# Three more mirrored score blocks per batch through VectorE, a planned number of score pairs per step, and casting loads of v and z

## The chip, the cores and the metric

The kernel runs on one core of one Trainium2 chip. The metric is the device time of one execution in microseconds, as the median of several runs. TensorE does the matrix products, VectorE, ScalarE and GpSimd (POOL in the profile) the elementwise work, and DMA queues, of which SyncE's (SP) is the main one, the loads, stores and transposes.

## The reference, cut to what matters

Two blocks follow each other, for 8 batches of 3200 tokens with 256 features.

```python
# u, v: (8, 3200, 256), z: (8, 3200, 64), all float32
scores = (1 / S) * z @ z.transpose(0, 2, 1)      # (8, 3200, 3200), symmetric
attn = np.maximum(scores, 0) ** 2                # symmetric too
x = u * (attn @ v)                               # (8, 3200, 256)

wq, wk = x @ w_q, x @ w_k                        # (8, 3200, 64)
W_tok = (1 / 8) * einsum('bsd,btd->bst', wq, wk)
mixed = einsum('bst,btd->bsd', W_tok, x)         # linear: wq @ (wk.T @ x)
out = np.maximum(mixed, 0) @ w_out
```

The score matrix is symmetric, so a block of it that is computed once can serve a second time as its transpose.

## The kernel before, in words

**Tiles.** A batch has 25 row tiles of 128 tokens (`NT`) and seven column groups: six of 512 tokens and a last one of 128 (`widths`, `NG`, `LASTG`). A score tile is 128 rows by 512 columns in fp16 for one row tile `ti` and one group `gi`; in the narrow group up to four row tiles share one. The list `tiles` holds all of them in the order in which they are made, and `ends` says where a group's tiles end. `is_turned(gi, gj)` says that the block of group `gi` with the four row tiles of group `gj` is made once and its mirror image, the block of `gj` with the rows of `gi`, comes by transposing. Ten blocks of a batch are such: those with `gj` at most two groups after `gi`, and (0, 4). The tiles of the mirror images are left out of `tiles`.

**A score pair.** Two tiles are made together by `scores` (L274): each contracts over 64 features of z, so one runs on the lower and one on the upper half of TensorE's rows, into one PSUM tile of two banks. There are three such PSUM tiles (`pps`), and projections, mixes and outputs take theirs from the same three. `first_stage` (L294) applies the relu and a scale into an fp32 tile `g`, on VectorE or ScalarE; `second_stage` (L304) squares it into the fp16 tile `at`, on POOL or ScalarE. For tiles of a turned block, `second_stage` also issues a DMA transpose from SP's queue (L329) into a tile `tt`.

**The second product.** `second_product` (L442) accumulates attn @ v for one group in two PSUM banks, reading its left operand from `at` or `tt` (`weights`, L434). When a group closes, `gate` (L466) multiplies by u into `x_sb`. Projections, heads, mixes and output products of the second block (`projections`, `heads`, `mix`, `proj_items`) are slipped between.

**Steps.** The main loop (L943) runs in steps `k`. Each step makes score pairs for later use, squares those of the step before (`waiting`), and does a part of the second product of the current group with tiles made at least `LAG` = 2 steps earlier. The loop makes three pairs per step, or two when a mix is done. How many rows of the second product a step takes follows from a heuristic at L1018 to L1032. One fixed pair of a step has its first stage on ScalarE (`act_pair`), the others on VectorE; of the second stages, fixed ones go to ScalarE. Each engine runs its instructions in the order in which they are written here.

**Loads.** The opening casts the first batch's v on the way by DMAs from POOL's queue (`load_first_v`, L111). For later batches `load_piece` (L140) loads pieces of v and z as fp32 by SP's queue into one of three staging tiles, and four or five steps later POOL or ScalarE, in turn, casts them to fp16 (L147):

```python
        def cast():
            copy = nc.gpsimd.tensor_copy if now[0] % 2 == 0 else nc.scalar.copy
            copy(out=dst()[:, n0 : n0 + nn, :], in_=piece[:])
```

`group_begun` (L794) says in which steps these loads are issued. The opening and the ending are written out by hand as lists of words.

Of the kernel before, what the change touches and what calls it, by code (L numbers as in the profile page):

```python
# [9 lines left out]
FP16 = mybir.dt.float16  # L10
# [6 lines left out]
def kernel(  # L17
# [31 lines left out]

    NAT = 11  # L50

    consts = ctx.enter_context(tc.tile_pool(name="consts", bufs=1))
# [86 lines left out]

    def load_piece(k, b, src, dst, n0, nn, later):  # L140
        d = src.shape[2]
        piece = pst.tile([P, nn, d], FP32, tag="piece", name="piece")
        nc.sync.dma_start(out=piece[:], in_=rows(src, b)[:, n0 : n0 + nn, :])

        def cast():
            copy = nc.gpsimd.tensor_copy if now[0] % 2 == 0 else nc.scalar.copy
            copy(out=dst()[:, n0 : n0 + nn, :], in_=piece[:])  # L147

        due(k + later, lambda: asides.append(cast))

    def load_v(k, b, n0, nn):
        if n0 == 0:
            vs[b] = pv.tile([P, NT, D], FP16, tag="v_sb", name="v_sb")
        load_piece(k, b, v, lambda: vs[b], n0, nn, 4 if b == 1 else 5)

    def load_z(k, b, n0, nn):
        load_piece(k, b, z, lambda: zr, n0, nn, 4)

# [18 lines left out]
    def spread_z(b, half, n0, n1):  # L177
        low, high = slice(0, dqk), slice(dqk, P)
        if half == 0:
# [53 lines left out]
    def is_turned(gi, gj):  # L233
        return gi < gj < LASTG and (gj <= gi + FAR or (gi, gj) == (0, 4))

# [58 lines left out]
    def first_stage(p0, sc, on_act):  # L294
        g = pg.tile([P, 2, W], FP32, tag="g", name="g")
        if on_act:
            nc.scalar.activation(out=g[:], in_=sc[:], func=RELU, scale=GSCALE)  # L297
        else:
            nc.vector.tensor_scalar(  # L299
                out=g[:], in0=sc[:], scalar1=0.0, scalar2=GSCALE, op0=AOP.max, op1=AOP.mult  # L300
            )
        return g

    def second_stage(p0, g, on_act):  # L304
        at = pat.tile([P, 2 * W], FP16, tag="at", name="at")
        out = at[:].rearrange("p (a w) -> p a w", a=2)
        if on_act:
            nc.scalar.square(out=out, in_=g[:])  # L308
        else:
            nc.gpsimd.tensor_mul(out=out, in0=g[:], in1=g[:])  # L310
# [7 lines left out]
        if len(blocks) == 2 and blocks[0][:3] == blocks[1][:3] and blocks[1][3] == blocks[0][3] + 1:  # L318
            blocks = [blocks[0][:4] + (2, blocks[0][5], blocks[1][6])]
        for b, gi, gj, n0, nn, c0, c1 in blocks:  # L320
            if (b, gi, gj) not in turned:
                bufs = {1: 3, 2: 4, 4: 1}[gj - gi]
                turned[b, gi, gj] = ptt.tile(
                    [P, 4, 4, P], FP16, tag=f"tt{gj - gi}", name=f"tt{gj - gi}", bufs=bufs
                )
# [5 lines left out]
        return turns  # L331

    accs = {}
# [132 lines left out]
    def gate(b, gi):  # L466
# [6 lines left out]
        ug = us.pop((b, gi))[:].rearrange("p n d -> p (n d)")  # L473
        n = min(2, nn) * D
        if is_split(b, gi):
            both = pg.tile([P, 2, W], FP32, tag="g", name="gt")
# [39 lines left out]
    def projections_out(b, gi, out):  # L516
        gw = widths[gi]
        if gi < LASTG:
            qks[b, gi] = pq.tile([P, W], FP16, tag="qk", name="qk")
        else:  # L520
            qks[b, gi] = pq.tile([P, P], FP16, tag="ql", name="ql", bufs=2)
        nc.scalar.copy(out=qks[b, gi][:, 0:gw], in_=out)  # L522

    def turn_keys(b, gi):
# [25 lines left out]

    def heads_out(b, gis, ps):
        if gis[0] == 0:
            hacc[b] = psml.tile([P, D], FP32, tag="ha", name="ha")
# [8 lines left out]

    def spread_heads(b):
        nc.scalar.copy(out=hss[b][dh:P, :], in_=hss[b][0:dh, :])
        nc.scalar.copy(out=hz[b % 2][dh:P, :], in_=hss[b][0:dh, :])
# [43 lines left out]
    def mix_out(b, pair, db, ps, on_dve=False):  # L609
        if db == 0:  # L610
# [3 lines left out]
            rts[b, pair, "both"] = both  # L614
        out = rts[b, pair, "both"][:, :, db, :]
        if on_dve:
            nc.vector.tensor_scalar(
# [46 lines left out]
    def proj_out(b, gi, src, ways):  # L664
# [8 lines left out]
        for on_dve, queue, n in ways:  # L673
            sl = slice(at * D, (at + n) * D)
            part = src[at // 2][:, 0 : n * D] if isinstance(src, list) else src[:, sl]
            if on_dve:
# [117 lines left out]
    def group_begun(k, b, gi):  # L794
# [4 lines left out]
        if gi == 0 and b + 1 < B:  # L799
            for i, (n0, nn) in enumerate([(0, 16), (16, NT - 16)]):  # L800
                at = k + (5 if b == 0 else 1) + i
                due(at, lambda at=at, n0=n0, nn=nn: load_z(at, b + 1, n0, nn))
            for i, n0 in enumerate((0, 5, 9)):
# [9 lines left out]
            for i in range(-(-NT // 4)):  # L813
                at = k + (9 + 5 * i // 3 if b == 0 else 4 + 2 * i)
                due(at, lambda at=at, i=i: load_v(at, b + 1, 4 * i, min(4, NT - 4 * i)))

# [29 lines left out]
    def key_due(k):  # L846
# [8 lines left out]
        begin = k + steps - 1  # L855
        if not todo_proj and not todo_mix and begin - k < 3 and begin - keyed_at[0] > 3:
# [80 lines left out]
    group_begun(1, 0, 0)  # L937
    steps = 6
    across = False
    left, first_sizes = [], [4, 5, 5, 5]  # L940
    gate_pending = False
    ahead = []
    while groups:  # L943
# [11 lines left out]
        if mix_due(k):  # L955
# [4 lines left out]
        n = min(n, NTILE - produced)  # L960
        pairs = list(range(produced, produced + n, 2))
        on_lanes = k >= 3 and len(pairs) + bool(mixing) >= 2
        keying = not mixing and key_due(k)
# [16 lines left out]
        staged = []  # L980
        act_pair = 0 if (gate_pending or k < 4) else 1
# [7 lines left out]
        if len(waiting) == 3:  # L989
            second_on_act = [False, True, k % 2 == 0]  # L990
        else:
            second_on_act = [False, True]
        seconds = [(p0, g, a) for (p0, g), a in zip(waiting, second_on_act) if g is not None]
        acts = [x for x in seconds if x[2]]
# [17 lines left out]
        if begins:  # L1012
# [4 lines left out]
            left = [t for t in range(NT) if t not in scored]  # L1017
        need = ends[b, gi]  # L1018
        rest = len(left) + sum(len(tis) for _, _, tis in tiles[consumed:need])
        if first_sizes:  # L1020
            size = first_sizes.pop(0)
            steps = len(first_sizes) + 1
        else:
            soon = [ready, made_by[k - 1], produced, produced + 5]
            steps = max(sum(need > x for x in soon) + 1, -(-rest // (25 if gi == LASTG else 13)))
            size = -(-rest // steps)
        closes = steps == 1
        new = min(ready, ends[b, gi]) - consumed
        if not closes:
            most = size + 3 if gi == LASTG else size  # L1030
            while new and sum(len(x[2]) for x in tiles[consumed : consumed + new]) > most:
                new -= 1  # L1032
        rows_ = [t for _, _, tis in tiles[consumed : consumed + new] for t in tis]
# [14 lines left out]
        if on_lanes:  # L1048
# [50 lines left out]
            todo = [(x, lambda lead, p0=p0: stage(p0, scores(p0, lead))) for x, p0 in zip(at_, between_)]  # L1099
# [161 lines left out]
```

## Time and profile before

| | |
|---|---|
| median of 3 runs | 778.56 us (778.5 to 779.31) |
| span of the profiled execution, first to last instruction | 776.9 us |
| TensorE busy | 765.0 us (98%) |
| VectorE / ScalarE / POOL busy | 474.0 / 558.4 / 554.1 us |
| granted TensorE clock, mean | 0.998 |

The profiled execution has no time of its own beside its span; the median of the runs stands 1.66 us above that span. In the groups of the profile a line reads: line, engine, operation, output tile, input tile, shapes, number of instructions, then busy microseconds, mean nanoseconds of one, and the idle time of the engine before them with what ended it.

### The profile page before, as it was taken

The numbers are of one execution on the slowest core, as the hardware profiler recorded it, in microseconds if no ns is written. First come the engines' busy times: TensorE is split into PE (matmuls) and PEld (weight loads), VectorE is DVE, ScalarE is ACT, GpSimd is POOL, SyncE is SP. The second block draws the span as 40 slices with busy tenths as digits, with TensorE's granted clock in tenths as the row PEclk, the third lists the DMA queues.
The fourth block names the chain that finished last, engine by engine and source line by source line (L and its number), as shares of the span: only waits on it lengthen the run. The fifth ranks groups of instructions, "written<-read, shape, count | busy, mean of one in ns | idle before, by whom it ended". The sixth has DMA issues, their size and how long they took to land.

```text
span 776.9 us, 28324 instructions
## 1 busy us (share of the span) xinstructions
PE 765.0 (98%) x12542; PEld 629.3 (81%) x12542; DVE 474.0 (61%) x459; ACT 558.4 (72%) x657; POOL 554.1 (71%) x361
## 2 busy tenths in 40 slices
PE   9999999999999999999999999999999999999996
PEld 6777877888788988888888887888888888988884
DVE  7654676546765577555766457655585646665444
ACT  8666787777778787685867667758687878685465
POOL 7897797768766678766879668886777546875450
PEclk9999999999999999999999999999999999999999
DMA  8899799987999679994999949999489995987726
GB/s 186 176 202 227 141 212 173 191 181 125 213 220 216 133 188 204 234 229 134 189 224 231 220 131 203 226 202 242 115 210 187 217 236 112 206 190 160 161 65 259
DMA packets 276554, 147.03 MB, mean 189 GB/s; under 512 B 252112, under 2 KB 255696, under 8 KB 276432
## 3 DMA queue, kind: packets, MB, share of 16 engines
q1 hardware_dynamic: 275712, 143.33, 87.8%
q0 software_dynamic: 576, 1.64, 1.1%
q8 instruction: 98, 1.61, 0.9%
q14 instruction: 24, 0.20, 0.1%
q10 hardware_dynamic: 144, 0.26, 0.1%
HBM read 59.38 MB, written 26.21 MB: 110 GB/s over the span
## 4 chain that ended last, share of the span: by engine, by line
PE 92%; DVE 2%; ACT 2%; POOL 1%; DMA 1%; issue 1%; ACTq 0%; DVEq 0%; POOLq 0%
PE acc L347 67%; PE sc L285 12%; PE qk L347 6%; PE fo L347 5%; PE mx L600 1%; POOL at L310 1%; DMA tt<-at 1%; DVE g L299 1%; DVE x_sb L485 1%; ACT at L308 1%; DVE fo L1219 0%; ACT g L297 0%; DMA z<-in_z_dram 0%; ACT gt L484 0%; DVE zT L136 0%
## 5 line engine op out<-in xcount | busy, mean ns | idle before, releaser
L299 DVE TENSOR_SCALAR g<-sc 128x1024 f32<-128x1024 f32 x337 | 410.1, 1223 | 242.1 <-PE sc L285 220.8
L310 POOL TENSOR_TENSOR at<-g 128x1024 f16<-128x1024 f32 x238 | 448.1, 1893 | 122.2 <-DVE g L299 93.6
L347 PE MATMUL acc<-v_sb,at 64*128 64x256 f16 (+1 forms) x7387 | 479.5, 269 | 2.0 <-DVE x_sb L485 0.7
L347 PEld LDWEIGHTS <-at 64*128 64x128 f16 (+1 forms) x7387 | 370.2, 94 | 84.3 <-PE acc L347 24.5
L308 ACT ACTIVATE at<-g 128x1024 f16<-128x1024 f32 x230 | 239.3, 1055 | 27.2 <-DVE g L299 16.0
L347 PE MATMUL acc<-v_sb,tt 64*128 64x256 f16 (+1 forms) x2540 | 179.2, 269 | 0.0
L285 PE MATMUL sc<-zT 64*128 64x512 f16 (+1 forms) x1104 | 170.3, 345 | 0.9 <-DVE g L299 0.5
L297 ACT ACTIVATE g<-sc 128x1024 f32<-128x1024 f32 x131 | 134.1, 1023 | 41.6 <-PE sc L285 39.5
L347 PEld LDWEIGHTS <-tt 64*128 64x128 f16 (+1 forms) x2540 | 129.5, 94 | 15.2
L487 POOL TENSOR_TENSOR x_sb<-gt,u_sb 128x512 f16<-128x512 f32 x48 | 61.2, 1275 | 71.5 <-ACT gt L484 56.6
L621 ACT ACTIVATE rt<-mx 128x1024 f16<-128x1024 f32 x47 | 47.9, 1024 | 30.8 <-PE mx L600 30.5
L285 PEld LDWEIGHTS <-zT 64*128 64x128 f16 x1104 | 57.3, 94 | 10.9 <-issue 3.2
L484 ACT COPY gt<-acc 128x512 f32<-128x512 f32 x48 | 28.1, 586 | 48.4 <-PE acc L347 48.2
L347 PE MATMUL fo<-wo,rt 64*128 64x256 f16 (+1 forms) x688 | 58.6, 270 | 0.0
L347 PE MATMUL qk<-x_sb,kx 64*128 64x256 f16 x368 | 55.7, 269 | 0.6 <-DVE g L299 0.6
L522 ACT CAST qk<-qk 128x512 f16<-128x512 f32 x47 | 27.5, 585 | 35.9 <-PE qk L347 35.8
L485 DVE TENSOR_TENSOR x_sb<-acc,u_sb 128x512 f16<-128x512 f32 x48 | 33.1, 690 | 26.1 <-PE acc L347 24.7
L347 PEld LDWEIGHTS <-rt 64*128 64x128 f16 (+1 forms) x688 | 36.6, 94 | 14.3 <-PE fo L347 5.2
L682 ACT ACTIVATE fo<-fo 128x1024 f32<-128x1024 f32 x39 | 39.9, 1023 | 4.3 <-PE fo L347 4.3
L347 PEld LDWEIGHTS <-kx 64*128 64x128 f16 (+1 forms) x386 | 35.7, 94 | 5.1 <-PE qk L347 0.2
L347 PE MATMUL qk<-xT_sb,wqk 64*128 64x512 f16 (+1 forms) x94 | 27.9, 377 | 0.0
L347 PE MATMUL qk<-xT_sb,wkq 64*128 64x512 f16 (+1 forms) x90 | 26.7, 376 | 0.4 <-ACT g L297 0.4
(79 smaller groups left out, 243.3 us busy)
## 6 DMA issues: line engine op xcount, KB each, us to landing
u_sb<-in_u_dram SPq DMA_DIRECT2D x48, 512.0 KB, 5.1
out_dram<-fo SPq DMA_DIRECT2D x43, 512.0 KB, 3.5
piece<-in_v_dram SPq DMA_DIRECT2D x42, 512.0 KB, 4.6
piece<-in_z_dram SPq DMA_DIRECT2D x7, 512.0 KB, 5.3
tt<-at SPq DMA_TRANSPOSE x162, 4.8
out_dram<-fo SPq DMA_DIRECT2D x9, 256.0 KB, 3.1
piece<-in_z_dram SPq DMA_DIRECT2D x7, 288.0 KB, 6.1
u_sb<-in_u_dram SPq DMA_DIRECT2D x8, 128.0 KB, 3.1
```

What stands on the lines that cost most here:

```text
L285: nc.tensor.matmul(out=sc[:, h, at : at + w], lhsT=zT[b][half : half + dqk, ds(z_at(b, h) + ti * P, P)], rhs=zT[b][half : half + dqk, ds(z ...
L297: nc.scalar.activation(out=g[:], in_=sc[:], func=RELU, scale=GSCALE)
L299: nc.vector.tensor_scalar(out=g[:], in0=sc[:], scalar1=0.0, scalar2=GSCALE, op0=AOP.max, op1=AOP.mult)
L308: nc.scalar.square(out=out, in_=g[:])
L310: nc.gpsimd.tensor_mul(out=out, in0=g[:], in1=g[:])
L347: return nc.tensor.matmul(out=self.out, lhsT=self.lhsT(rows), rhs=self.rhs(rows), start=start, stop=stop)
L484: nc.scalar.copy(out=upper[:], in_=accs[1][:])
L485: nc.vector.tensor_mul(out=x[:, 0:n], in0=accs[0][:, 0:n], in1=ug[:, 0:n])
L487: nc.gpsimd.tensor_mul(out=x[:, n : 2 * n], in0=upper[:], in1=ug[:, n : 2 * n])
L522: nc.scalar.copy(out=qks[b, gi][:, 0:gw], in_=out)
L621: nc.scalar.activation(out=out, in_=ps[:], func=RELU)
L682: nc.scalar.mul(out=flat_out[:, sl], in_=part, mul=FINAL_SCALE)
```

## The change

Three parts.

First, three more blocks per batch, (0, 3), (1, 4) and (2, 5), are mirrored. Their transposes are not made by DMA. `turn_blocks` lets VectorE transpose the 32x32 pieces of a tile within each group of 32 partitions into a tile `t1`, and `move_block` then moves the pieces to their place, sixteen copies of 32 partitions by 512 fp16 elements for each block. `vector_jobs` slips these jobs behind the first stages. The transposed tiles `tt` come from one list of eleven, `tt_free`, in which a tile returns when all its readers have been written out.

Second, steps are planned ahead. `STEPS` says how many steps each group of each batch takes, `plan` derives from that how many tiles each step's product consumes, and `pairs_now` makes as many pairs as the following steps need on average. Which engine does a first or second stage is chosen by a running estimate (`busy`, `free`, `clock`) of when VectorE, ScalarE and POOL become free.

Third, v and z of later batches are loaded by casting DMAs from POOL's queue, straight into their fp16 tiles; the staging tiles and the casts go. One of the seven `g` tiles goes too.

```diff
     NAT = 11
+    NTT = 11
+    BY_VECTOR = {(0, 3), (1, 4), (2, 5)}
+    STEPS = [
+        [4, 3, 3, 3, 2, 3, 1],
+        [4, 4, 3, 3, 2, 3, 1],
+        [4, 4, 3, 3, 3, 3, 1],
+        [5, 4, 3, 3, 3, 3, 1],
+        [5, 3, 4, 3, 2, 3, 2],
+        [4, 4, 3, 3, 3, 3, 1],
+        [5, 3, 4, 3, 2, 3, 2],
+        [4, 5, 3, 3, 2, 4, 1],
+    ]
-    pst = ctx.enter_context(tc.tile_pool(name="pst", bufs=3))
-    pg = ctx.enter_context(tc.tile_pool(name="pg", bufs=7))
+    pg = ctx.enter_context(tc.tile_pool(name="pg", bufs=6))
+    pt1 = ctx.enter_context(tc.tile_pool(name="pt1", bufs=1))
...
+    def load_v(b, n0, nn):
+        if n0 == 0:
             vs[b] = pv.tile([P, NT, D], FP16, tag="v_sb", name="v_sb")
+        nc.gpsimd.dma_start(out=vs[b][:, n0 : n0 + nn, :], in_=rows(v, b)[:, n0 : n0 + nn, :])
+        busy("P", 550)
+
+    def load_z(b, n0, nn):
+        nc.gpsimd.dma_start(out=zr[:, n0 : n0 + nn, :], in_=rows(z, b)[:, n0 : n0 + nn, :])
+        busy("P", 550)
...
     def is_turned(gi, gj):
-        return gi < gj < LASTG and (gj <= gi + FAR or (gi, gj) == (0, 4))
+        return gi < gj < LASTG and (
+            gj <= gi + FAR or (gi, gj) == (0, 4) or (gi, gj) in BY_VECTOR
+        )
...
+    def busy(engine, ns):
+        free[engine] = max(free[engine], clock[0]) + ns
+
+    def sooner(ways):
+        return min(ways, key=lambda w: max(free[w[0]], clock[0]) + w[1])[0]
...
+    def turn_blocks(b, gi, gj, n0, nn, c0, at):
+        key = b, gi, gj
+        if key not in t1s:
+            while moves:
+                moves.pop(0)()
+            t1s[key] = pt1.tile([P, 4, 4, 4, P // 4], FP16, tag="t1", name="t1"), []
+        t1, seen = t1s[key]
+        busy("D", 600 * nn)
+        nc.vector.transpose(
+            out=t1[:, :, n0 : n0 + nn, :, :].rearrange("p r n a t -> p (n a) r t"),
+            in_=at[:, c0 : c0 + nn * W].rearrange("p (x r t) -> p x r t", r=4, t=P // 4),
+        )
+        seen.extend(range(nn))
+        if len(seen) == 4:
+            moves.extend(lambda q=q, r=r: move_block(key, q, r) for q in range(4) for r in range(4))
+
+    def move_block(key, q, r):
+        if key not in turned:
+            turned[key] = turned_tile(*key)
+        n = P // 4
+        busy("D", 200)
+        nc.vector.tensor_copy(
+            out=turned[key][ds(r * n, n), :, :, ds(q * n, n)].rearrange("p n a t -> p (n a) t"),
+            in_=t1s[key][0][ds(q * n, n), r, :, :, :].rearrange("p n a t -> p (n a) t"),
+        )
+
+    def vector_jobs(until):
+        while by_vector and now[0] - by_vector[0][0] >= 2:
+            by_vector.pop(0)[1]()
+        while (by_vector or moves) and max(free["D"], clock[0]) < until:
+            by_vector.pop(0)[1]() if by_vector and not moves else moves.pop(0)()
...
+    def pairs_now(k, most):
+        j = k - 3
+        rate = 0
+        for i in range(j, len(upto)):
+            need = upto[min(i + LAG, len(upto) - 1)]
+            rate = max(rate, (need - produced) / (i - j + 1))
+        n = 2 * int(-(-rate // 2))
+        n = max(min(n, most), must_make(k))
+        assert n <= most, (k, n, most)
+        room = (upto[j - 1] if j else consumed) + 2 * NAT - produced
+        return max(0, min(n, room - room % 2, NTILE - produced))
...
         def stage(p0, sc):
-            on_act = len(staged) == act_pair and not mixing
-            staged.append((p0, first_stage(p0, sc, on_act)))
+            way = sooner([("D", 1250), ("A", 1050)])
+            staged.append((p0, first_stage(p0, sc, way == "A")))
+            vector_jobs(clock[0] + 1800)
...
+        for p0, g in waiting:
+            if g is not None:
+                a_end, p_end = (max(spent[e], clock[0]) + t for e, t in (("A", 1080), ("P", 1910)))
+                on_act = a_end + 500 < p_end
...
         each(late)
+        turned_read(b, gi, rows_)
+        clock[0] = begun_at + step_ns
+        vector_jobs(clock[0] + 500)
```

More of the change, by code (lines that the diff above doesn't have):

```diff
@@ L295, in first_stage @@
         g = pg.tile([P, 2, W], FP32, tag="g", name="g")
+        busy("A" if on_act else "D", 1050 if on_act else 1250)
         if on_act:
@@ L522, in projections_out @@
         nc.scalar.copy(out=qks[b, gi][:, 0:gw], in_=out)
+        busy("A", 600 if gi < LASTG else 270)
     def turn_keys(b, gi):
@@ L615, in mix_out @@
         out = rts[b, pair, "both"][:, :, db, :]
+        busy("D" if on_dve else "A", 1250 if on_dve else 1040)
         if on_dve:
@@ L937, with plan, must_make @@
     group_begun(1, 0, 0)
-    steps = 6
+    def plan():
+        sizes, news, at = [], [], 0
+        for b, gi in groups:
+            n, n_old = ends[b, gi] - at, 0
+            todo = sum(len(tis) for _, _, tis in tiles[at : ends[b, gi]])
+            n_old = NT - todo
+            if (b, gi) == (0, 0):
+                parts = [4, 5, 5, 5]
+                n, todo, at = n - consumed, todo - consumed, consumed
+            else:
+                m = STEPS[b][gi]
+                parts = [(NT * (i + 1)) // m - (NT * i) // m for i in range(m)]
+            done, rows_done = 0, 0
+            for i, size in enumerate(parts):
+                rows_done += size
+                to = -(-n * rows_done // sum(parts))
+                news.append(at + to)
+                sizes.append((size, len(parts) - i))
+            at = ends[b, gi]
+        return sizes, news
+    def must_make(k):
+        n = max(0, upto[min(k - 3 + LAG, len(upto) - 1)] - produced)
+        return n + n % 2
+    def pairs_now(k, most):
[9 more added lines that the diff above has]
+        return max(0, min(n, room - room % 2, NTILE - produced))
     across = False
-    left, first_sizes = [], [4, 5, 5, 5]
+    left = []
+    sizes, upto = plan()
+    clock[0] = 25000.0
     gate_pending = False
@@ L1017 @@
             left = [t for t in range(NT) if t not in scored]
[L1018 to L1026, printed above, removed]
-        closes = steps == 1
[L1028 to L1032, printed above, removed]
+        size, steps = sizes[k - 3]
+        closes = steps == 1
+        new = upto[k - 3] - consumed
+        assert upto[k - 3] <= ready, (k, b, gi)
         rows_ = [t for _, _, tis in tiles[consumed : consumed + new] for t in tis]
@@ L1098, with staged_at @@
                 across = not across
-            todo = [(x, lambda lead, p0=p0: stage(p0, scores(p0, lead))) for x, p0 in zip(at_, between_)]
+            def staged_at(x, lead, p0):
+                clock[0] = begun_at + x * step_ns
+                stage(p0, scores(p0, lead))
+            todo = [(x, lambda lead, x=x, p0=p0: staged_at(x, lead, p0)) for x, p0 in zip(at_, between_)]
             for x in acts[1:]:
```

68 lines of the change are left out of this document (40 added, 28 removed).

## The prediction

> **What bounds the kernel now.** I read the page from the top: how busy each engine is, then what makes up the chain that ended last, then whether that holds in every stretch.
>
> ```profile
> span 776.9 us, 28324 instructions
> ...
> PE 765.0 (98%) x12542; PEld 629.3 (81%) x12542; DVE 474.0 (61%) x459; ACT 558.4 (72%) x657; POOL 554.1 (71%) x361
> ...
> PE 92%; DVE 2%; ACT 2%; POOL 1%; DMA 1%; issue 1%; ACTq 0%; DVEq 0%; POOLq 0%
> ...
> 0.00:25.00 25.00, 23.32 (x279) 16.65 (x281) 18.61 (x22) 20.66 (x23) 19.24 (x21) 1.00 0.79 168
> 25.00:745.00 720.00, 716.65 (x12016) 593.44 (x12014) 442.98 (x421) 520.16 (x611) 530.56 (x339) 1.00 0.92 190
> 745.00:776.90 31.90, 25.01 (x255) 19.25 (x251) 12.42 (x18) 17.57 (x25) 4.35 (x3) 0.96 0.51 182
> ```
>
> TensorE is busy for 98% and carries 92% of the chain. The three windows (columns: length, then PE, PEld, DVE, ACT, POOL, clock, DMA share) show where the rest is: between 25 and 745 us PE idles 3.35 of 720 us, at the full clock. So the steady part is TensorE work laid end to end; the DMA engines, at 0.92 there, do not hold it up. A change in that part pays what it takes from TensorE, as long as nothing else becomes late. The median of the runs, 778.56 us, is 1.66 us above the span of the profiled execution; I make the sum on the span and add that 1.66.
>
> **What the change takes from TensorE.** Count the score tiles. A batch without mirroring has 6 x 25 wide tiles and 7 for the narrow last group, 157. Ten mirrored blocks save 4 each: 117 per batch, 936 in all, 468 pairs. The rows agree: 337 + 131 first stages.
>
> ```profile
> L299 DVE TENSOR_SCALAR g<-sc 128x1024 f32<-128x1024 f32 x337 | 410.1, 1223 | 242.1 <-PE sc L285 220.8
> ...
> L297 ACT ACTIVATE g<-sc 128x1024 f32<-128x1024 f32 x131 | 134.1, 1023 | 41.6 <-PE sc L285 39.5
> ...
> 740.33 0.22 PE sc L285 x2
> ...
> 301.12 0.38 PE L285 MATMUL sc<-zT 64*128 64x512 f16 x2
> 301.34 0.82 PE L347 MATMUL acc<-v_sb,at 64*128 64x256 f16 x12
> ```
>
> Thirteen blocks leave 105 tiles per batch, 420 pairs: 48 fewer. A pair (two matmuls, one on each half of the rows) lasts 0.38 us in the timeline, but the next product starts 0.22 us after it, and the chain charges 0.22 too. So TensorE loses 48 x 0.22 = 10.6 us. The second product is unchanged in number; it only reads a turned block where it read a made one. The step table of the change sums to 169 steps, so a step is about 766/169 = 4.5 us.
>
> **What it adds on VectorE.** 24 blocks, each with two transposes of 128x1024 fp16 and 16 moves of 32x512 fp16: 48 and 384 instructions. Neither exists in the trace. The nearest rows:
>
> ```profile
> L121 DVE CAST zd<-z 128x512 f16<-128x512 f32 x1 | 0.4, 420 | 0.0
> L121 DVE CAST zd<-z 128x256 f16<-128x256 f32 x1 | 0.3, 294 | 2.0 <-DMA z<-in_z_dram 2.0
> L121 DVE CAST zd<-z 128x448 f16<-128x448 f32 x1 | 0.6, 609 | 0.0
> L136 DVE COPY zT<-ztp 128x1024 f16<-128x1024 f16 x1 | 0.7, 691 | 0.0
> ```
>
> A transpose of 1024 elements lies between 0.69 us (the fp16 copy of that size) and 1.22 us (the first stage of that size); I take 1.22, since nothing shows that a transpose gets the copy's rate: 59 us. A move of 512 elements: 0.42 us is the cast of that size from fp32, 0.29 the one with half the elements and so the same bytes read. I take 0.29, since the move reads 2-byte elements: 111 us, or 161 at 0.42. Back go up to 48 first stages of 1.22, 59 us. VectorE so comes to between 474 - 59 + 59 + 111 = 585 and 474 + 59 + 161 = 694 us, 76% to 90% of 766. It fits on average, beside TensorE, and I cost it at nothing while its cover holds. [...]
>
> The cover is the slack of a first stage. Every score pair, projection and mix needs one of three two-bank PSUM tiles.
>
> ```profile
> L621 ACT ACTIVATE rt<-mx 128x1024 f16<-128x1024 f32 x47 | 47.9, 1024 | 30.8 <-PE mx L600 30.5
> L522 ACT CAST qk<-qk 128x512 f16<-128x512 f32 x47 | 27.5, 585 | 35.9 <-PE qk L347 35.8
> L682 ACT ACTIVATE fo<-fo 128x1024 f32<-128x1024 f32 x39 | 39.9, 1023 | 4.3 <-PE fo L347 4.3
> ```
>
> That is 468 + 47 + 47 + 39 = 601 tiles in 776.9 us, one per 1.29 us; with three of them a tile may live 3.88 us. Less 0.38 for the scores and 1.22 for the first stage, a first stage may be 2.3 us late before TensorE waits. After the change there are 553 in 766 us, and the slack is 4.16 - 1.60 = 2.6 us. A block's VectorE work is 2 x 1.22 + 16 x 0.29 = 7.1 us, while VectorE's idle 39% is 1.8 us of a step: each block loads about four steps, 96 of the 169. The plan tops VectorE up to 1.8 us ahead and gives the next first stage to ScalarE when that would end sooner, so by its own numbers lateness stays under 2.6 us.
>
> **What it moves between engines and queues.**
>
> ```profile
> L147 POOL CAST v_sb<-piece 128x1024 f16<-128x1024 f32 (+1 forms) x25 | 23.4, 935 | 0.0
> L147 ACT CAST v_sb<-piece 128x1024 f16<-128x1024 f32 (+1 forms) x24 | 22.9, 955 | 0.0
> L112 POOL DMA_DIRECT2D v_sb<-in_v_dram x4 | 2.3, 579 | 0.1
> 304.15 0.57 SPq L143 DMA_DIRECT2D piece<-in_v_dram  x1
> piece<-in_v_dram SPq DMA_DIRECT2D x42, 512.0 KB, 4.6
> v_sb<-in_v_dram POOLq DMA_DIRECT2D x1, 512.0 KB, 6.1
> q0 software_dynamic: 576, 1.64, 1.1%
> ```
>
> Each of 7 batches loads v in 7 pieces and z in 2: 63 issues of 0.57 us leave SP's queue (36 us), so the transposes behind them go earlier; 63 issues of 0.579 us join POOL's (36 us) and its casts go (23.4 us and the few for z), about even. ScalarE loses its casts, over 22.9 us. All of this lies beside TensorE: priced at nothing. A casting load lands after 6.1 instead of 4.6 us, but is issued several steps of 4.5 us before its first reader. The opening's four casting loads of v took 1.1% of the DMA engines' time for a whole batch, so seven more batches are 8%, in place of the plain loads. Second stages fall by 48 as well, off ScalarE or POOL.
>
> **The sum.** 776.9 - 10.6 = 766.3. New waits of TensorE: from zero to the tens of us of the rivals below; I take as much again as the steady part has now, 3.4 us, because the plan balances the engines by costs that lie near the rows but with VectorE a good deal fuller. 769.7, and 1.66 outside the span: 771.4 us.
>
> **Rivals.**
>
> *VectorE's moves are held up by POOL (slower).* The moves are the first steady VectorE instructions that read and write SBUF alone, and POOL is 71% busy with instructions like this:
>
> ```profile
> L310 POOL TENSOR_TENSOR at<-g 128x1024 f16<-128x1024 f32 x238 | 448.1, 1893 | 122.2 <-DVE g L299 93.6
> POOL at L310 <- DVE g L299: 93.6, 87, 4.4
> ```
>
> If the two engines exclude each other for whole instructions, a move that comes upon a running one waits 0.95 us on average, 0.67 us with POOL's share; and since POOL waited for VectorE before only 87 of 238 second stages, the next one often stands ready to slip in between two moves, for 1.89 us. In a loaded stretch VectorE has nothing left to work that off with, so the first stages behind the moves slip by the sum. A block stands 2.6 us; the gain of 10.6/24 = 0.44 us per block is gone at 3.0 us, 1.6 POOL instructions per block of 16 moves. With two, 3.8 us, TensorE waits 1.2 us per block: 24 x 1.2 = 29 us, 776.9 - 10.6 + 29 + 1.7 = 797 us; with more it grows by 45 us for each. For it speaks the share of POOL; against it, that the trace has no such case: L299 reads PSUM. Its one hint is weak: the cast of 448 elements took 609 ns, longer than that of 512 with 420. [...] No run here shows it yet. I give this 0.30.
>
> *A transpose waits for its second stage (about no change).* The plan may put a transpose on VectorE in the step in which POOL is only given the square it reads. It then blocks VectorE for up to 1.89 us, and 1.22 of its own makes 3.1: TensorE loses 0.5 us. For all 48 that is 26 us, for half of them 13: 776.9 - 10.6 + 13 + 1.7 = 781 us. Against it: a step earlier the square is mostly done. 0.13.
>
> *The plan also removes today's waits (faster than forecast).* Fewer pairs per step and no casts on ScalarE or POOL might take away the 3.35 us: 776.9 - 10.6 - 3.4 + 1.7 = 764.6 us. 0.07.
>
> *The blocks are not saved,* because the plan makes the same pairs: no, the saving is in the list of tiles itself, so I give it no chance of its own.
>
> **The numbers.** The forecast has 0.50, with a range of its own from 767 to 776 (no new waits with some of the old gone, to 8 us of new ones). A measurement of this kernel tells 0.2%, 1.6 us, from no change. Faster: 0.50, 0.07 and a little of the second rival, 0.58. Within 0.2% (777.0 to 780.1): 0.06, from the second. Slower: 0.36. The range for 8 in 10 starts at 764, where the last rival lies, and goes to 800, which takes in the first rival up to two POOL instructions per block; about 0.17 is left above.
>
> **What would show it.** Right: 420 first stages over L299 and L297; PE busy near 755 us and still 98%; a move near 0.29 us with little spread; VectorE's waits still mostly for the scores. Wrong by the first rival: moves with a mean well above 0.4 us and a maximum near 1.9, and PE's idle before L285 released by VectorE's first stage. Wrong by the second: VectorE's transposes waiting for L310 in sum over 20 us. If PE shows neither and still idles, it waits for something I have not priced, a load of z or v or a turned block's tile.

## The result, and the profile after

| | before | after |
|---|---|---|
| median of the runs | 778.53 us | 938.5 us (933.19 to 940.15) |
| ratio | | 1.203, 95% interval 1.198 to 1.208 |
| span of the profiled execution | 776.9 us | 937.6 us |
| TensorE busy / idle in the span | 765.0 / 11.9 us | 802.9 / 134.7 us |
| mean granted TensorE clock | 0.998 | 0.938 |

The change costs a fifth of the time. The page of the kernel after, from the head, the busy times and the chain:

```profile
span 937.6 us, 28428 instructions
...
PE 802.9 (86%) x12478; PEld 659.0 (70%) x12478; DVE 648.0 (69%) x810; ACT 566.5 (60%) x661; POOL 471.5 (50%) x342
...
PE 59%; DVE 30%; issue 6%; ACT 3%; DMA 1%; POOL 1%; DVEq 0%; ACTq 0%; POOLq 0%
PE acc L408 45%; DVE tt L383 16%; DVE g L302 9%; PE sc L287 6%; PE qk L408 4%; PE fo L408 3%; DVE t L370 2%; DVE x_sb L549 2%; ACT at L312 1%; PE mx L667 1%; ACT g L300 1%; DMA xTl<-xl 1%; DVE ha L622 0%; POOL at L314 0%; ACT rt L689 0%
```

No engine is full. TensorE's part of the chain has gone from 92% to 59%, and 30% is now VectorE, more than half of that on line 383, the moves. The pairs were saved as planned: 256 + 164 = 420 first stages. Yet TensorE is busier than before, 802.9 us against 765.0. So the 160.7 us of longer span are 122.8 us more idle TensorE and 37.9 us more busy time. The clock accounts for the second part: the trace lists 20 stretches at half clock, 115.5 us in all. In these, pairs of matmuls of 256 columns start 0.213 us apart (median), 0.109 at the full clock. TensorE is busy for 77.2 us of them and so loses half of that, 38.6 us. The 10.6 us of the saved pairs do not show in the busy time; the last sections return to this.

The instructions that are new on VectorE, beside the first stage, by groups:

```profile
L302 DVE TENSOR_SCALAR g<-sc 128x1024 f32<-128x1024 f32 x256 | 308.9, 1218 | 154.2 <-PE sc L287 148.6
L383 DVE COPY tt<-t 32x512 f16<-32x512 f16 x384 | 220.5, 574 | 6.7
L370 DVE STREAM_TRANSPOSE t<-at 128x1024 f16<-128x1024 f16 x48 | 58.4, 1230 | 8.0 <-POOL at L314 4.1
```

The spread of the moves, from the view of line 383 (minimum, median and maximum in ns):

```profile
L383 DVE COPY tt<-t x384: 260/286/4310, 27.9 to 877.5; 32x512 f16<-32x512 f16 x192
```

The transposes cost what was forecast. A move has a median of 286 ns, as forecast, but a mean of 574: (574 - 286) x 384 = 111 us are in a part of them, up to 4.3 us each. Where they are can be read from the timeline, VectorE first, then POOL, then the waits of TensorE (all of the kernel after):

```profile
126.75 2.36 DVE L302 TENSOR_SCALAR g<-sc 128x1024 f32<-128x1024 f32 x2
129.14 5.35 DVE L383 COPY tt<-t 32x512 f16<-32x512 f16 x4
134.52 1.22 DVE L302 TENSOR_SCALAR g<-sc 128x1024 f32<-128x1024 f32 x1
...
129.19 3.89 POOL L314 TENSOR_TENSOR at<-g 128x1024 f16<-128x1024 f32 x2 [3.20 <-DVE g L302]
133.04 1.30 POOL L551 TENSOR_TENSOR x_sb<-gt,u_sb 128x512 f16<-128x512 f32 x1
...
135.80 0.27 PE L408 MATMUL qk<-x_sb,kx 64*128 64x256 f16 x1 [4.50 <-DVE g L302]
```

Four moves take 5.35 us, just as long as POOL's two squares and its multiplication beside them, from 129.19 to 134.34. The first stage behind the moves starts at 134.52, its score tile comes free at 135.7, and TensorE, which stands before a matmul into such a tile, has waited 4.50 us. Counted in the trace, 80 of the 384 moves last over 0.39 us, and every one of these ends 0.09 to 0.16 us after an instruction of POOL.

TensorE's waits on VectorE (total us, times, longest):

```profile
PE sc L287 <- DVE g L302: 59.9, 26, 7.8
PE acc L408 <- DVE x_sb L549: 43.5, 22, 5.6
```

And two windows of 20 us, in which the third figure from the end is TensorE's granted clock:

```profile
60.00:80.00 20.00, 11.15 (x142) 8.59 (x142) 16.96 (x23) 7.47 (x9) 8.61 (x12) 0.74 0.59 94
...
200.00:220.00 20.00, 19.89 (x360) 17.82 (x358) 8.26 (x8) 11.01 (x14) 9.71 (x7) 1.00 0.39 80
```

Two kinds of wait: for the first stage that frees a score tile, and for the multiplication by u at a group's end (`x_sb`), which frees the accumulator. Before the change the first was 0.5 us in all and the second 0.7:

```profile
PE acc L347 <- DVE x_sb L485: 0.7, 4, 0.2
...
PE sc L285 <- DVE g L299: 0.5, 1, 0.5
```

And where TensorE pauses, its clock sinks: 0.74 in the window with 8.85 us of idle time, 1.00 in the one without.

### The profile page after: what moved, and what is told of

Same layout as the page of the kernel before. It is cut to its first block, busy times and chain, and to the rows that moved or that the text cites. A ratio compares the mean times of both kernels' runs of the same rounds, so it can differ in the third digit from the quotient of the medians.

```text
span 937.6 us, 28428 instructions
## 1 busy us (share of the span) xinstructions
PE 802.9 (86%) x12478; PEld 659.0 (70%) x12478; DVE 648.0 (69%) x810; ACT 566.5 (60%) x661; POOL 471.5 (50%) x342
## 4 chain that ended last, share of the span: by engine, by line
PE 59%; DVE 30%; issue 6%; ACT 3%; DMA 1%; POOL 1%; DVEq 0%; ACTq 0%; POOLq 0%
PE acc L408 45%; DVE tt L383 16%; DVE g L302 9%; PE sc L287 6%; PE qk L408 4%; PE fo L408 3%; DVE t L370 2%; DVE x_sb L549 2%; ACT at L312 1%; PE mx L667 1%; ACT g L300 1%; DMA xTl<-xl 1%; DVE ha L622 0%; POOL at L314 0%; ACT rt L689 0%
## 5 line engine op out<-in xcount | busy, mean ns | idle before, releaser
L314 POOL TENSOR_TENSOR at<-g 128x1024 f16<-128x1024 f32 x188 | 356.9, 1901 | 325.7 <-DVE g L302 180.7
L408 PE MATMUL acc<-v_sb,at 64*128 64x256 f16 (+1 forms) x6623 | 462.5, 279 | 51.2 <-DVE x_sb L549 43.5
L408 PEld LDWEIGHTS <-at 64*128 64x128 f16 (+1 forms) x6623 | 355.2, 97 | 130.1 <-issue 53.5
L302 DVE TENSOR_SCALAR g<-sc 128x1024 f32<-128x1024 f32 x256 | 308.9, 1218 | 154.2 <-PE sc L287 148.6
L300 ACT ACTIVATE g<-sc 128x1024 f32<-128x1024 f32 x164 | 167.1, 1023 | 172.5 <-PE sc L287 167.8
L408 PE MATMUL acc<-v_sb,tt 64*128 64x256 f16 x3328 | 237.0, 274 | 0.0
L383 DVE COPY tt<-t 32x512 f16<-32x512 f16 x384 | 220.5, 574 | 6.7
L287 PE MATMUL sc<-zT 64*128 64x512 f16 (+1 forms) x1008 | 159.2, 350 | 65.7 <-DVE g L302 59.9
L408 PEld LDWEIGHTS <-tt 64*128 64x128 f16 x3328 | 175.6, 96 | 18.2
L370 DVE STREAM_TRANSPOSE t<-at 128x1024 f16<-128x1024 f16 x48 | 58.4, 1230 | 8.0 <-POOL at L314 4.1
```

The source lines that it names most:

```text
L287: nc.tensor.matmul(out=sc[:, h, at : at + w], lhsT=zT[b][half : half + dqk, ds(z_at(b, h) + ti * P, P)], rhs=zT[b][half : half + dqk, ds(z ...
L302: nc.vector.tensor_scalar(out=g[:], in0=sc[:], scalar1=0.0, scalar2=GSCALE, op0=AOP.max, op1=AOP.mult)
L370: nc.vector.transpose(out=t1[:, :, n0 : n0 + nn, :, :].rearrange("p r n a t -> p (n a) r t"), in_=at[:, c0 : c0 + nn * W].rearrange("p (x ...
L383: nc.vector.tensor_copy(out=turned[key][ds(r * n, n), :, :, ds(q * n, n)].rearrange("p n a t -> p (n a) t"), in_=t1s[key][0][ds(q * n, n), ...
L408: return nc.tensor.matmul(out=self.out, lhsT=self.lhsT(rows), rhs=self.rhs(rows), start=start, stop=stop)
```

## The experiments

All are compared with the kernel before on the same chip, whose median was between 778.42 and 778.81 us each time; a run's figure is its median with the ratio to that kernel and the 95% interval. "Theory 1" is that the moves wait for POOL.

**The three blocks by DMA.**

```diff
-            if (gi, gj) in BY_VECTOR:
+            if False:
```

> The changed kernel with one edit: the three extra blocks are turned by DMA transposes from SP's queue like the other ten, so VectorE has neither transposes nor moves; the plan, the casting loads and the 48 fewer score pairs stay. Theory 1 (VectorE's moves wait for POOL's running instruction, first stages behind them are late, TensorE stands still and its clock sinks): with no moves the loss is gone, 768 to 776 us, TensorE's clock back near 1.00. Rival A (the plan of the steps itself starves TensorE, for instance pairs made too late): stays above 900 us. Rival B (48 more transposes overload SP's queue and the DMA engines): 785 to 850 us, with TensorE waiting for at or tt tiles.

Measured: 815.59 us, 1.044 (1.038 to 1.050). Without VectorE's jobs 123 us are gone, TensorE's clock is back at 0.988, so rival A falls. But theory 1's 768 to 776 us is missed: rival B is true as well. The DMA queues of its page, and its longest wait for a DMA:

```profile
q1 hardware_dynamic: 317328, 127.24, 84.2%
q0 software_dynamic: 9648, 15.98, 14.3%
```

```profile
POOL at L314 <- DMA tt<-at: 112.3, 30, 8.3
```

Two queues take 98.5% of the DMA engines' time, and POOL waits 112 us before a square until a transpose has read the `at` tile that it would overwrite. ScalarE waits another 48 us for the same reason. TensorE's own waits are for VectorE and ScalarE, 10.2 us at most in one group, so that the DMA engines bound this kernel by way of POOL and ScalarE is likely, but not tested by itself. This is a reason why a route through VectorE may be wanted at all.

**The same moves for nobody, in two forms.** Here the DMA turns the blocks and VectorE does all its jobs into a spare tile. First with the copies as they are:

```diff
-                continue
...
-            out=turned[key][ds(r * n, n), :, :, ds(q * n, n)].rearrange("p n a t -> p (n a) t"),
+            out=t2s[key][ds(r * n, n), :, :, ds(q * n, n)].rearrange("p n a t -> p (n a) t"),
```

> The changed kernel, with the three blocks turned by DMA as in the run before, but VectorE still does all its transposes and all 384 moves of 32x512, into a spare tile that nobody reads (one tile less in the list of turned tiles, ten for eleven). Theory 1: the moves still wait for POOL, mean near 0.57 us, maximum above 4 us, and the time stays near the changed kernel's, 880 to 945 us. Rival C (what costs the time is that TensorE waits for the turned blocks to be complete, not that VectorE is late for the first stages): near 775 us, since no one waits for the moves' output.

Then with each copy replaced by a short transpose, of 32x128 fp16 elements:

```diff
-        nc.vector.tensor_copy(
-            out=t2s[key][ds(r * n, n), :, :, ds(q * n, n)].rearrange("p n a t -> p (n a) t"),
-            in_=t1s[key][0][ds(q * n, n), r, :, :, :].rearrange("p n a t -> p (n a) t"),
+        nc.vector.transpose(
+            out=t2s[key][ds(r * n, n), 0, :, ds(q * n, n)],
+            in_=t1s[key][0][ds(q * n, n), r, 0, :, :],
         )
```

> [...] Theory 1: no waits for POOL, every one of the 384 near 0.29 us with little spread, and 768 to 785 us. Rival D (VectorE is simply too full, and the plan prices a move at 200 ns where it takes 286): as slow as the run before, above 880 us, since the number and the length of the instructions are the same.

Measured: 938.37 us, 1.203 (1.195 to 1.210), and 825.64 us, 1.058 (1.052 to 1.064). The group of these instructions in the first run, then in the second, and their spread in the second:

```profile
L383 DVE COPY t<-t 32x512 f16<-32x512 f16 x384 | 220.5, 574 | 6.7
```

```profile
L383 DVE STREAM_TRANSPOSE t<-t 32x128 f16<-32x128 f16 x384 | 115.4, 301 | 6.1
```

```profile
L383 DVE STREAM_TRANSPOSE t<-t x384: 256/303/308, 28.0 to 762.8; 32x128 f16<-32x128 f16 x192
```

The plan, the instruction counts and, nearly, the unhindered lengths (286 and 303 ns) are the same. The kind of instruction differs, and with it the data: a transpose here moves a quarter of the bytes. (The run with 4-byte transposes below moves all of them.) The copies have the outliers, the transposes a maximum of 308 ns, and the difference is 113 us. Rival C falls with the first run: no one reads the spare tile, and it is as slow as the changed kernel, so the loss does not come from the blocks being complete too late. Rival D falls with the second. The second stays above theory 1's 785 us. Its trace shows two things left: POOL waits 84 us for the DMA transposes, as in the run before (815.59), and TensorE waits 20 us for `x_sb`. What each costs is not shown.

**The moves priced at what they take.**

```diff
-        busy("D", 200)
+        busy("D", 300)
```

> The changed kernel with one number changed: the plan prices a move at 300 ns in place of 200, which is what an unhindered move takes (median 286). Rival D (underpriced moves make VectorE late): most of the loss goes, below 830 us. Theory 1: the waits for POOL stay, 100 us or more over the 384 moves; moves come in smaller clumps, so some of the loss may go, but the time stays above 880 us.

Measured: 937.99 us, 1.202 (1.195 to 1.209). Nothing is won; the mean of a move is 651 ns there. An honest price for an unhindered move does not help a plan that does not know of POOL. A price at the mean length, waits included, was not run.

**VectorE's route with 4-byte transposes in place of the copies.** Each move is a 32x32 transpose of 4-byte words over the same 32x512 fp16 elements (256 words), and the three blocks come by VectorE again, without extra DMA transposes. The blocks so reach their tiles in a wrong order; all else is computed.

```diff
-        busy("D", 200)
-        nc.vector.tensor_copy(
-            out=turned[key][ds(r * n, n), :, :, ds(q * n, n)].rearrange("p n a t -> p (n a) t"),
-            in_=t1s[key][0][ds(q * n, n), r, :, :, :].rearrange("p n a t -> p (n a) t"),
+        busy("D", 400)
+        nc.vector.transpose(
+            out=turned[key][ds(r * n, n), :, :, ds(q * n, n)].rearrange("p n a t -> p (n a) t").bitcast(mybir.dt.uint32),
+            in_=t1s[key][0][ds(q * n, n), r, :, :, :].rearrange("p n a t -> p (n a) t").bitcast(mybir.dt.uint32),
         )
```

> [...] The plan prices such a move at 400 ns; I estimate 0.42 us, from the rate and the fixed part of the transposes already measured. Theory 1 (the loss is the moves' wait for POOL): every move near 0.42 us with little spread although it is longer than an unhindered copy, TensorE's clock near 1.0, 770 to 800 us. Rival D (VectorE has too much to do): VectorE's own work is now 52 us more than unhindered copies would be, so it stays above 850 us.

Measured: 812.21 us, 1.043 (1.040 to 1.046), span 809.0. The spread of these instructions, and TensorE's longest waits:

```profile
L383 DVE STREAM_TRANSPOSE tt<-t x384: 411/436/443, 27.8 to 757.6; 32x256 uint32<-32x256 uint32 x192
```

```profile
PE acc L408 <- DVE x_sb L549: 19.4, 31, 1.8
PE sc L287 <- DVE g L302: 5.6, 13, 0.8
```

Each is half as long again as an unhindered copy, and the kernel is 126 us faster than the changed one: what hurts is not the length but the waiting. (The price of 400 ns is a second difference; the run at 300 ns showed nothing for the price.) The clock is 0.999. No TensorE wait of either kind is over 1.8 us any more, where they went to 7.8 in the changed kernel; its longest idle stretch of any kind is 2.7 us. TensorE is busy for 765.3 us here, 37.6 less than in the changed kernel with the same products, which is what half clock cost there by the count above (38.6). But 812 is above the 770 to 800 expected. Further runs look for the rest.

**Casting loads alone, on the kernel before.**

```diff
-        load_piece(k, b, v, lambda: vs[b], n0, nn, 4 if b == 1 else 5)
+        nc.gpsimd.dma_start(out=vs[b][:, n0 : n0 + nn, :], in_=rows(v, b)[:, n0 : n0 + nn, :])
```

> The kernel before with one part of the change alone: v and z by casting DMAs from POOL's queue, with no staging tiles and no casts on ScalarE and POOL; same steps, same ten blocks. By the traces the plain loads took about 127 us of the DMA engines' time and the casting ones about 109, so nothing is slower there; TensorE's work is the same: 774 to 780 us, no change. If the casting loads hold back POOL or land too late for their readers: above 785 us.

Measured: 779.67 us, 1.0018 (0.9999 to 1.0037): no difference that can be told, as expected. Its estimate of the DMA engines' time was off, though:

```profile
q1 hardware_dynamic: 266640, 114.65, 76.2%
q0 software_dynamic: 9648, 15.98, 15.5%
```

Against 87.8% and 1.1% before, the plain loads took about 90 us (682 less 592), the casting ones 112 us (120 less the opening's 8.5): the casting loads cost the DMA engines more, not less.

**Plan and casting loads without the three blocks.**

```diff
-    BY_VECTOR = {(0, 3), (1, 4), (2, 5)}
+    BY_VECTOR = set()
...
-        n = 6
+        n = 8
...
-            n = 4
+            n = 6
```

> The changed kernel without the three extra blocks (an empty set, and up to eight tiles a step where six were allowed, so that the plan comes out with 468 pairs): plan and casting loads alone. If the plan is sound, it is as fast as the kernel before, 774 to 785 us. If the plan starves TensorE by itself (rival A), above 800 us; then part of the loss in the changed kernel belongs to it.

Measured: 787.57 us, 1.011 (1.009 to 1.014), a little over the range given. The plan, with the casting loads, costs some 9 us; it does not starve TensorE on the scale of the loss. Rival A has a small truth.

**One block per batch by DMA.**

```diff
-    BY_VECTOR = {(0, 3), (1, 4), (2, 5)}
+    BY_VECTOR = {(0, 3)}
...
-            if (gi, gj) in BY_VECTOR:
+            if False:
...
-        n = 6
+        n = 8
...
-            n = 4
+            n = 6
```

> The changed kernel with one extra block per batch, (0, 3), turned by DMA from SP's queue, none by VectorE (and up to eight tiles a step). A transpose takes about 2.8 us of all DMA engines (133 us more on SP's queue for 48 of them in the run with three blocks by DMA), so 16 of them take 44 us and the DMA engines come to about 716 us, under TensorE's time; TensorE does 16 pairs less, 3.5 us. If the plan is sound: 770 to 778 us, which would beat both kernels. If the DMA engines bound it already: 785 to 800 us.

Measured: four runs between 793.74 and 816.22 us, with a median of 802.78 us, 1.031 (1.025 to 1.036). Even the two shortest, 793.74 and 799.51 us, are 1.023 times the kernel before in the mean. So 770 to 778 us is missed, and these two lie in the 785 to 800 us of the other case: 16 more transposes make the kernel at least 6 us and in these two some 9 us slower than the run without them (787.57), though TensorE has 16 pairs less to do. The DMA queues of the shortest one, and POOL's wait for them:

```profile
q1 hardware_dynamic: 283536, 118.85, 80.0%
q0 software_dynamic: 9648, 15.98, 14.8%
```

```profile
POOL at L314 <- DMA tt<-at: 73.5, 20, 6.9
```

At 94.8% of their time on average the DMA engines are late often enough to hold back POOL's squares. An average below one hid a bound.

**The wait by itself.**

```python
meet(); moves()
meet(); squares(8)
meet(); squares(8); moves()
meet(); squares(8); words()
meet()
for i in range(4):
    load(i); squares(1)
moves()
```

(The body of a small kernel that computes nothing of the reference, calls joined on lines: `meet` makes both engines wait for each other, `moves` are VectorE's 16 copies of a block, `squares(8)` eight squares of 128x1024 on POOL, `words` the 16 transposes of 32x256 4-byte words, `load` a casting load.)

> [...] Theory 1, in the sharp form that the trace of the changed kernel suggests (a move waits to the end of the instruction that POOL runs, and one move comes in between two of POOL's): alone a move takes 0.29 us and a square 1.9; together the first eight or nine moves take about 1.9 us each and the rest 0.29, some 17 us for the 16 where they take 4.6 alone, and POOL's squares become longer by little; the transposes take 0.43 us each beside the squares as well. [...] If the two only share bandwidth, the moves become evenly longer.

Measured, from the timeline (start, duration, engine), with both engines released together before each stretch:

```profile
4.12 4.76 DVE L57 COPY d<-t 32x512 f16<-32x512 f16 x16
...
9.83 15.69 POOL L71 TENSOR_TENSOR p<-a 128x1024 f16<-128x1024 f32 x8
...
26.07 18.20 DVE L57 COPY d<-t 32x512 f16<-32x512 f16 x16
26.17 15.74 POOL L71 TENSOR_TENSOR p<-a 128x1024 f16<-128x1024 f32 x8
...
44.98 7.43 DVE L64 STREAM_TRANSPOSE d<-t 32x256 uint32<-32x256 uint32 x16
45.08 15.70 POOL L71 TENSOR_TENSOR p<-a 128x1024 f16<-128x1024 f32 x8
...
61.33 13.73 DVE L57 COPY d<-t 32x512 f16<-32x512 f16 x16
```

Sixteen moves take 4.76 us alone and 18.20 beside eight squares; the squares take 15.69 and 15.74. VectorE pays all of it. 18.20 is what the sharp form gives, and the records of the single moves show it: one of 0.28 us that starts ahead of POOL's first square, eight of 1.87 to 1.94 us, seven of 0.28 to 0.29 us. The transposes take 7.43 us, 16 times 0.46, beside the same squares: no wait. In the last stretch POOL issues four casting loads and four squares in turn from 61.41 to 71.43; the moves end at 75.06. Again one move of 0.28 us starts ahead of POOL; then there are four of 2.42 to 2.57 us, and eleven unhindered ones after POOL's end. So one move came in per load and square together, and none between a load and its square.

**The group's end kept free.**

```diff
-        while (by_vector or moves) and max(free["D"], clock[0]) < until:
+        while (by_vector or moves) and max(free["D"], clock[0]) < until and sizes[k - 3][1] > 1:
...
+            left.sort(key=lambda t: (group_of(t), gi) in BY_VECTOR)
```

(With a third edit that does open jobs before the step that reads them, all on top of the 4-byte transposes, now priced at 430 ns.)

> The run with 4-byte transposes in place of moves (812 us), with three edits to the plan: VectorE gets no such jobs in a step that closes a group, rows from these blocks are taken last by the product, and jobs still open are done before the step that reads them. What is left of the loss there: the product of the next group waits for the multiplication by u on VectorE at the close (19.4 us in 31 waits), which has no spare buffer. Theory 2 (that wait, and the pauses around it, are most of the 25 us by which that run is above the one with the plan alone, 787.6): 780 to 795 us, with under 5 us of that wait left. If the rest is only VectorE's fullness in the other steps: 805 to 815 us.

Measured: 799.94 us, 1.027 (1.022 to 1.032), 12 us less than without the edits; the wait for `x_sb` went from 19.4 to 11.3 us. That lies between the two expectations, and the wait did not fall under the 5 us that theory 2 asked for. The three edits together take away half of the 25 us, and the waits for `x_sb` fell by 8.1 us; which edit did it is not shown.

**The moves by ScalarE, and by POOL.** Two attempts to keep the computation and lose the wait, both with the three edits above:

```diff
-        busy("D", 200)
-        nc.vector.tensor_copy(
+        busy("A", 600)
+        nc.scalar.copy(
```

> The whole computation, with the same three edits to the plan, and the moves made by ScalarE (priced 600 ns) in place of VectorE. By theory 1 ScalarE's moves do not wait for POOL: each near 0.6 us with little spread, 384 of them 225 us; ScalarE is then near 85% full, and the plan gives VectorE and POOL more of the stages. 775 to 800 us; below 777 would beat the kernel before. If ScalarE becomes the bound, above 810 us, with TensorE waiting for ScalarE's first stages.

```diff
-    pt1 = ctx.enter_context(tc.tile_pool(name="pt1", bufs=1))
+    pt1 = ctx.enter_context(tc.tile_pool(name="pt1", bufs=2))
...
-        busy("D", 200)
-        nc.vector.tensor_copy(
+        busy("P", 560)
+        nc.gpsimd.tensor_copy(
```

> The whole computation, with the three edits to the plan, and the moves made by POOL itself (priced 560 ns), with two t1 tiles in place of one and ten turned tiles for eleven, so that VectorE's next transposes need not wait for the moves. [...] Theory 1: POOL's moves take about 0.56 us each whatever VectorE does, 384 of them 215 us, which brings POOL to about 88% of the span; TensorE no longer waits for VectorE, 780 to 805 us. If POOL becomes the bound (its squares and the multiplication by u late, and the turned blocks late for the product): above 820 us. If two t1 tiles do not take away the wait that the run with ScalarE's moves showed, VectorE's transposes wait for POOL for more than 50 us.

Measured: 936.29 us, 1.202 (1.198 to 1.206), and 803.21 us, 1.030 (1.022 to 1.039). The longest wait on the movers in the first, then the group of the moves in the second:

```profile
DVE t L370 <- ACT tt L385: 83.2, 16, 10.8
```

```profile
L385 POOL COPY tt<-t 32x512 f16<-32x512 f16 x384 | 233.3, 608 | 45.3 <-DVE t L370 28.7
```

The first is a miss. ScalarE's moves took 615 ns on average and 618 at most, near the 0.6 us expected and with no outliers, but I had overlooked the single `t1`: VectorE's next transpose waits until ScalarE has read it, 83 us in all, and the first stages wait behind it as before (TensorE waits up to 7.6 us for one). The waits are others than in the changed kernel, so that the two times are alike looks like chance. With two `t1` tiles and POOL as mover this wait is not among VectorE's any more, and the time is in the range expected. The two runs differ in the mover as well, so that the second `t1` made the difference is likely but not shown. No run beats the kernel before: the plan's 9 us and the 10.6 us counted for TensorE nearly cancel, and every route tried for the blocks costs more than what remains.

## Why the prediction was wrong

**The saving was right in number and near in size, but the sign named for it was not.** There are 420 pairs, 48 fewer. TensorE's busy time does not fall to the 755 us expected: it is 765.3 us in the run with 4-byte transposes, at a clock of 0.999, as against 765.0 before and 767.6 in the run with the plan alone. Busy time counts each matmul's whole record, 0.27 us for one of 256 columns, though in a full stretch the next pair of them starts 0.106 us after the last, so a short wait can lie inside it. Counting each with 0.106 us per 256 columns instead, I estimate from the two traces 748.8 us of work with the plan alone and 740.7 us with 4-byte transposes: some 8 us less where 10.6 were forecast.

**The lengths were right, and yet the cost was not.** 1.23 us for a transpose and 0.286 for an unhindered move, where I took 1.22 and 0.29. Moves and transposes were then costed at nothing "while its cover holds". The step that failed is this one: the cover did not hold, and the mean move took 574 ns. The mechanism was the one named as first rival and weighed 0.30: VectorE's copies held up by POOL. The pair of runs with the spare tile shows 113 us for it, the 4-byte transposes 126 us. The reason I gave against it, that the trace of before has no such case, was no reason: the kernel before had no steady VectorE copy of this kind, in which the wait could have been seen. The small kernel shows it: the sixteen moves take 18.20 us beside POOL's squares and 4.76 alone.

**The size of the rival was off too, in three terms.** First, the waits: 111 us over 24 blocks are 4.6 us per block, 2.4 lengths of a square where I took two, and the longest move took 4.31 us where I named 1.9. By my own formula, 4.6 - 2.6 = 2.0 us for each of 24 blocks, that is 49 us and 817 us in all, already out of the range. Second, the slack of 2.6 us per block holds for first stages alone. The multiplication by u at a group's end has none, because the accumulator has no second buffer; TensorE waited for it 43.5 us in the kernel after, and in the run without the copies the three edits, of which one keeps VectorE free there, brought 12 us. Third, the clock: a pause of TensorE costs more than itself, 38.6 us here. After the longest wait two score matmuls of 0.38 us took 0.61:

```profile
68.38 0.61 PE L287 MATMUL sc<-zT 64*128 64x512 f16 x2 [7.83 <-DVE g L302]
```

I had not put a price on that at all. With all three the sum comes to 817 + 43.5 + 38.6 = 899 us; the rest up to 938 is not assigned. Which pauses were followed by half clock can be counted. In all runs but the small kernel, TensorE's idle stretches of 3 us or more came with half clock (during them or at most 3.5 us after) 65 times of 66, those of 2 to 3 us 22 times of 35, those of 1.5 to 2 us once in 20; in the changed kernel alone it was 17 of 17, 2 of 3 and none of 4.

**The second rival** (a transpose that waits for its square) was weighed 0.13 and is small: 4.1 us of waits for POOL in the row of line 370. **The casting loads** were costed at nothing, and that was right for the time, 1.0018; the 8% of the DMA engines' time estimated for seven more batches came out as 14% in the run with casting loads alone (15.5% less 1.1%). **The DMA engines** were put aside with a share of 0.92 because TensorE was full; in the runs with more DMA transposes, at 94.8% and 98.5%, POOL waits for them 74 and 112 us, so they are the likely next bound, a few per cent away.

**What stays open.** The run with 4-byte transposes lies 44 us above 768 us (778.6 less 10.6); 9 belong to the plan and 12 to the three edits. The rest can be split, by spans, between the run with these edits (796.6 us) and the plan alone less 10.6 us (785.0 - 10.6 = 774.4): 22.2 us. Of these, 14.9 us are more idle TensorE, which waits 9.6 us more for `x_sb` (11.3 against 1.7) and 3.6 us more for first stages (4.0 against 0.4). The other 7.3 us are busy time, 764.3 us where 767.6 less 10.6 would be 757.0: a saving of about 8 us instead of 10.6 and short waits inside the busy time. Why VectorE is still late at a group's end is not shown.

## What to carry to other kernels

Before work is moved to an idle engine, ask what its neighbours run beside it, not only how long it is idle: the copies on VectorE beside a POOL that was 50% busy took twice their length on average (574 ns, where the median is 286), and what was written behind them was late with them: behind the four moves of 5.35 us a first stage came so late that TensorE stood for 4.50 us. Look at the maximum and the median of a group, not only its mean. For a kernel that is 98% TensorE, list for each engine which of its instructions TensorE has no spare buffer for; these have no slack, whatever the average says.

## What the runs showed of the hardware

The first rival asked what follows if VectorE's moves and POOL exclude each other; not expected there was how one-sided the wait is. In the small kernel POOL's eight squares took 15.74 us beside the moves and 15.69 without, the sixteen moves 18.20 us beside the squares and 4.76 without; VectorE got in one move between two squares, and one per load and square where POOL issued loads between them. In the changed kernel two moves fared worse still: each took 4.31 us, across a load and two squares. A VectorE transpose of 4-byte words over the same bytes went at 0.43 to 0.46 us with no wait at all beside the squares: of these two forms over the same bytes, only the copy waited. TensorE's half clock came in stretches of 3.41, 6.83 or 10.24 us in the changed kernel, but for the last one, which outlasts it.
